# A hand-written instruction order taken two chunks further, across a block border, in a three-layer kernel

## The chip, the cores and the metric

The kernel runs on one core of one Trainium2 chip. Time is device time in microseconds (us) of one execution, the median of several; lower is better.

## The reference

Three layers follow one another over 1,536 tokens of 512 numbers.

```python
# 1: attention, 2 x 8 heads, head size 64: a local window and block maxima as keys
scores_l = scale * np.matmul(q, k.transpose(0, 1, 3, 2))   # kept where |i - j| < 16
scores_s = scale * np.einsum('bhsd,bhnd->bhsn', q, k_sum) + np.log(32)
a = np.exp(scores_all - max);  a = a / (a.sum(-1) + 1e-9)
x = np.matmul(a, v_all)
# 2: dense layer with ELU, 512 -> 2048 -> 512
h = x @ w_in
g = np.where(h > 0.0, h, np.exp(np.minimum(h, 0.0)) - 1.0)
x = g @ w_out
# 3: top-1 of 8 experts, 512 -> 1024 -> 512, weighed by a softmax gate and a sigmoid gate
e_idx = np.argmax(x @ w_gate, axis=1)
out[mask] = gate_w * eom * (np.maximum(x[mask] @ w1[e], 0.0) @ w2[e])
```

## The kernel before, in words

The attention works in 24 units of 64 tokens. A unit is a chain: scores on TensorE (line 330), their maxima on VectorE (340), exp on ScalarE (353), sums, reciprocal (`add_eps` 385, `recip` 391) and norm (401), a turn on TensorE (412), its copy on ScalarE (419), and the product with v on TensorE (449). From the product, which lies in PSUM, ScalarE takes the high part of x (`x_hi`, 455) and VectorE the low part (`x_lo`, 462). From unit 8 on two units go through the chain together.

The dense layer works in four blocks of tokens, 512, 256, 384 and 384 wide, each made of the units that lie in it (8, 4, 6 and 6). Each block goes through 16 chunks of 128 of the 2,048 hidden numbers. A chunk is `mm_h` (line 482: twelve matmuls, high and low parts of x against high and low parts of the weights), `elu` (two passes on ScalarE at 495, two on VectorE at 502 and 508), the split of the result into `gh` (518, ScalarE) and `gl` (524, VectorE), the split of the chunk's output weights (`w_high` 175 on ScalarE, `w_low` 179 on VectorE), and `mm_y` (543), which adds the chunk into one PSUM bank for each 128 tokens: four banks in block 0, two in block 1. TensorE takes `mm_y` two chunks behind `mm_h`. When a block's last `mm_y` is done, `out_y` copies the banks out and stores them. Below, h(j,c) and Y(j,c) are `mm_h` and `mm_y` of block j, chunk c.

During block 0 the weights come in as 64-bit numbers and are put together as fp32: `load_w` (122), `conv_r` (130 and 134, ScalarE), `conv_t` (146, 147 or 149, VectorE), `conv_f` (156, VectorE, for chosen chunks GpSimd), and for w_in `conv_h` (162, ScalarE) and `conv_l` (167, VectorE). The means of v that the units from 12 on need are summed on VectorE (`mean_v1`, 239), go to DRAM and back by DMA, and are put at the top of v by `v_pad` (255). GpSimd has the short copies of k, some norms, and the constants of the routing (`route_consts`, 758 to 793): a load `rc` and some casts, which nobody reads before the first block's tokens are routed.

What sets the order. Until the end of block 0, all engines and the load queue (SP) follow one list, the string `START`, whose tokens are steps: a letter for the step and digits for the unit or chunk. `G` and `H` are `mm_h`, `Y` is `mm_y`, `U` and `V` are the two halves of `elu`, `g` and `f` the split of g, `i` and `j` that of the output weights, `t` the turn, `o` the product, `h` and `l` the parts of x, `F` and `K` sums, `L` a load. Small tables say which engine takes a step: `NE` (norm), `WE` and `KE` (copies of k), `PADA` (units whose `v_pad` is ScalarE's), `CP` (`conv_f` on GpSimd), `EXP` (subtraction of maxima on GpSimd), `RADD` (`add_eps` on GpSimd), `BITS` (w_in chunks converted by a shorter way on ScalarE and a longer one on VectorE). After block 0, TensorE's order is the order of a loop over the steps (`part1`); the table `PAIRS` gives for each pair of units from 12 on the half step at which its chain begins (two half steps a chunk, block 1 has 32 to 63). The other engines then take what a scheduler by priority gives them. The experts at the end are planned apart from that.

Of the kernel before, what the change touches and what calls it, by code (L numbers as in the profile page):

```python
# [13 lines left out]
U32 = mybir.dt.uint32  # L14
# [8 lines left out]
E, F2 = 8, 1024  # L23
# [17 lines left out]
QS = (0, 2, 6, 8)  # L41
C3 = 2
WARM = 56
BITS = (0, 1, 2, 3, 6, 8)
PAIRS = {12: 35, 14: 45, 16: 54, 18: 65, 20: 74, 22: 83}
AT = (2, 6, 8, 8)
LQ = 5
ER = 13
# [33 lines left out]
class Prog:  # L82
# [42 lines left out]
    def conv_r(self, c, part):  # L125
# [13 lines left out]
    def conv_t(self, c, part):  # L139
# [112 lines left out]
    def v_pad(self, u):  # L252
# [363 lines left out]
    def part1(self):  # L616
# [22 lines left out]
        steps = [(j, c) for j in range(NBLK) for c in range(NF)]  # L639
        todo = {}  # L640

        def at(hs, fn, *args):
            todo.setdefault(hs, []).append((fn, args))

        for j in range(2, NBLK):
            for n in range(UNITS[j]):
                u = U0[j] + n
                h0 = PAIRS[u - n % 2]
                if UPB <= u < UPB + self.NKV:
# [27 lines left out]
        h0 = 2 * NF * (NBLK - 1)  # L677
# [39 lines left out]
    def start_up(self):  # L717

        unit = dict(k=self.k_sum, s=self.scores, m=self.maxes, b=self.less_max, e=self.weights, z=self.sums, r=self.recip, R=self.recip2, n=self.norm, t=self.turn_of, c=self.turned,
                    o=self.weighted, h=self.x_hi, l=self.x_lo, p=self.v_pad, x=self.max_k0, w=self.window, a=self.add_eps, M=self.mean_v0, P=self.pad_v0, K=self.red_sum, F=self.mean_v1, Z=self.keep_warm)  # L720
        load = dict(k=self.load_k0, Q=self.load_q0, V=self.load_v0, W=self.load_kw, c=self.load_c, w=self.load_w, q=self.load_q, v=self.load_v, s=self.load_sum, u=self.load_v1)
        part = dict(A=self.conv_r, B=self.conv_t, C=self.conv_f, D=self.conv_h, E=self.conv_l)
        chunk = dict(U=self.elu_act, V=self.elu_dve, Y=self.mm_y, g=self.g_high, f=self.g_low, i=self.w_high, j=self.w_low)
        half = set()
        for u in range(NV):
            self.unit0(u)
        with self.tc.manual_schedule():
            for op in START.split():
# [838 lines left out]
```

## Time and profile before

| | |
|---|---|
| three runs | 526.79, 528.25 and 529.17 us, median 528.25 |
| the profiled execution | 526.98 us, of which 525.2 us are the span of the trace |
| TensorE (PE) busy | 511.6 us, 97% of the span |
| VectorE (DVE) busy | 337.1 us, 64% |
| ScalarE (ACT) busy | 305.1 us, 58% |
| GpSimd (POOL) busy | 54.4 us, 10% |

The shares are means over stages that differ: attention and the start of the dense layer until about 41 us, the rest of block 0 until about 131, block 1 until about 192, then blocks 2 and 3 with the routing, and the experts. They are to be read by stage. A timeline row gives start, duration, engine, line, operation and tiles, and in brackets the engine's idle time before it with what ended it.

### The profile page before, as it was taken

To read this page: it belongs to the slowest core of one execution; us is meant where nothing else is said; L and a number is where in the kernel's file an instruction comes from. 1 tells how busy PE (TensorE), PEld (TensorE's weight loads), DVE (VectorE), ACT (ScalarE), POOL (GpSimd) and SP (SyncE) were. 2 spreads that over 40 slices of the span, in tenths; PEclk is the share of its full clock that TensorE was granted. 3 is DMA by queue.
4 is the path that set the end of the run, shared out by engine and by line. 5 is a ranking of instruction groups with operands and counts; after the bars stand their busy time and mean duration, and the time that the engine had idled before them with its cause. 6 is when DMAs were issued, how large, how long until landed. Compare 5 with 4: busy or idle time off the path is not lost. (4 is left out here: it accounts for less than half of the span.)

```text
span 525.2 us, 9833 instructions
## 1 busy us (share of the span) xinstructions
PE 511.6 (97%) x3325; PEld 409.6 (78%) x3325; DVE 337.1 (64%) x945; ACT 305.1 (58%) x715; POOL 54.4 (10%) x102
## 2 busy tenths in 40 slices
PE   9999999998999999999999999999999999999994
PEld 6486778886888889888898897987888567576883
DVE  5899999997688868676557899668321011535410
ACT  3899998994677658656546547543232223656421
POOL 3530000001000000000000000113411111100001
PEclk9999999999999999999999999999999999999998
DMA  8999334551311212200001025310689898594601
GB/s 293 405 396 331 119 118 140 179 195 50 132 32 52 81 45 78 82 0 16 2 0 62 1 75 192 96 61 1 183 319 302 297 360 317 174 344 149 203 22 43
DMA packets 37131, 78.08 MB, mean 149 GB/s; under 512 B 3951, under 2 KB 9807, under 8 KB 37072
## 3 DMA queue, kind: packets, MB, share of 16 engines
q1 hardware_dynamic: 34752, 70.02, 39.2%
q0 software_dynamic: 2320, 7.34, 4.0%
q8 instruction: 28, 0.46, 0.4%
q14 instruction: 31, 0.25, 0.2%
HBM read 100.37 MB, written 6.55 MB: 204 GB/s over the span
## 5 line engine op out<-in xcount | busy, mean ns | idle before, releaser
L482 PE MATMUL h<-xh,wi 128*128 128x384 f32 (+2 forms) x528 | 142.8, 338 | 2.5 <-DVE elp L508 1.5
L543 PE MATMUL y<-wsp,gh 128*128 128x512 f32 x368 | 117.3, 400 | 0.0
L482 PEld LDWEIGHTS h<-xh,wi 128*128 128x128 f32 x528 | 94.5, 190 | 10.7 <-DVE elp L508 2.4
L482 PE MATMUL h<-xl,wi 128*128 128x384 f32 (+2 forms) x264 | 87.9, 333 | 1.6 <-DVE xl L462 1.6
L543 PEld LDWEIGHTS y<-wsp,gh 128*128 128x128 f32 x368 | 66.8, 190 | 12.3 <-issue 0.5
L543 PE MATMUL y<-wsp,gl 128*128 128x512 f32 x184 | 72.5, 394 | 0.0
L1222 DVE TENSOR_TENSOR holdl<-S,holdh 128x512 fp32r<-128x512 f32 x22 | 15.2, 690 | 72.5 <-ACT holdh L1218 53.7
L1190 PE MATMUL h<-w2s,holdh 128*128 128x512 f32 x176 | 59.8, 400 | 0.0
L1233 PE MATMUL y<-w2s,holdh 128*128 128x512 f32 x176 | 59.0, 398 | 0.0
L482 PEld LDWEIGHTS h<-xl,wi 128*128 128x128 f32 x264 | 50.2, 190 | 5.6 <-DVE xl L462 1.8
L502 DVE SCALAR_TENSOR_TENSOR elt<-ele,elt 128x384 f32<-128x384 f32 (+2 forms) x64 | 35.5, 554 | 24.6 <-ACT ele L495 24.3
L495 ACT ACTIVATE elt<-h 128x384 f32<-128x384 f32 (+2 forms) x64 | 31.2, 487 | 31.1 <-PE h L482 30.5
L175 ACT CAST wsp<-wo 128x512 fp32r<-128x512 f32 x62 | 38.0, 617 | 16.8 <-PE y L543 16.0
L179 DVE TENSOR_TENSOR wsp<-wo,wsp 128x512 fp32r<-128x512 f32 x62 | 42.6, 689 | 6.3 <-ACT wsp L175 6.0
L518 ACT CAST gh<-elp 128x384 fp32r<-128x384 f32 (+2 forms) x62 | 31.5, 508 | 23.5 <-DVE elp L508 12.8
L524 DVE TENSOR_TENSOR gl<-elp,gh 128x384 fp32r<-128x384 f32 (+2 forms) x62 | 34.0, 549 | 12.2 <-ACT gh L518 11.9
L543 PEld LDWEIGHTS y<-wsp,gl 128*128 128x128 f32 x184 | 34.7, 188 | 8.0 <-DVE gl L524 0.3
L353 ACT ACTIVATE e<-e,nb 128x120 f32<-128x120 f32 x88 | 33.6, 385 | 10.8 <-DVE nb L340 10.8
L1233 PEld LDWEIGHTS y<-w2s,holdh 128*128 128x128 f32 x176 | 33.1, 188 | 8.4 <-issue 1.6
L1190 PEld LDWEIGHTS h<-w2s,holdh 128*128 128x128 f32 x176 | 33.1, 188 | 8.2 <-ACT w2s L1258 0.8
L1264 DVE TENSOR_TENSOR w2s<-wo,w2s 128x512 fp32r<-128x512 f32 x48 | 30.8, 687 | 9.3 <-ACT w2s L1258 7.8
L508 DVE SCALAR_TENSOR_TENSOR elp<-elt,h 128x384 f32<-128x384 f32 (+2 forms) x64 | 35.1, 548 | 0.9
(290 smaller groups left out, 819.8 us busy)
## 6 DMA issues: line engine op xcount, KB each, us to landing
wo<-in_w SPq DMA_DIRECT2D x9, 2048.0 KB
wo<-in_w SPq DMA_DIRECT2D x18, 1024.0 KB
ri<-in_w_in SPq DMA_DIRECT2D x16, 512.0 KB
ro<-in_w_out SPq DMA_DIRECT2D x16, 512.0 KB
wo<-in_w SPq DMA_DIRECT2D x32, 256.0 KB
w2p<-in_w SPq DMA_DIRECT2D x32, 256.0 KB
w2q<-in_w SPq DMA_DIRECT2D x24, 256.0 KB
k<-in_kw SPq DMA_DIRECT2D x18, 192.0 KB
```

What stands on the lines that cost most here:

```text
L175: self.nc.scalar.copy(w[:, 0], self.w[c, 1].bitcast(F32))
L179: self.nc.vector.tensor_tensor(w[:, 1], self.w[c, 1].bitcast(F32), w[:, 0].bitcast(F32), op=ALU.subtract)
L353: nc.scalar.activation(e[:, p], e[:, p], AF.Exp, bias=nb[:, p:p + 1], scale=-1.0, accum_out=sm[:, p:p + 1])
L482: nc.tensor.matmul(h, lhsT=w[:, wl, k * 128:k * 128 + 128], rhs=x[:, k, a:b], start=(n == 0), stop=(n == 11))
L495: self.nc.scalar.activation(self.te[j, c][i], self.h[j, c], AF.Exp if i else AF.Tanh, scale=1.0 if i else 0.5)
L502: nc.vector.scalar_tensor_tensor(t, e, 1.0, t, op0=ALU.add, op1=ALU.mult)
L508: nc.vector.scalar_tensor_tensor(p, t, 0.0, h, op0=ALU.min, op1=ALU.max)
L518: self.nc.scalar.copy(gh, p)
L524: self.nc.vector.tensor_tensor(gl, p, gh.bitcast(F32), op=ALU.subtract)
L543: nc.tensor.matmul(self.y[j][t], lhsT=gx[:, sl], rhs=wx, start=(c == 0 and n == 0), stop=(c == NF - 1 and n == len(ops) - 1))
L1190: nc.tensor.matmul(self.h[s, hf], lhsT=x[:, k], rhs=w, start=(n == 0), stop=(n == 11))
L1233: nc.tensor.matmul(self.y2[s], lhsT=g[:, ks], rhs=w, start=(i == 0 and n == 0), stop=(i == 7 and n == 2))
```

## The change

- `START` is written anew, over its whole length. It goes on past block 0: h(1,0) and h(1,1) with their `elu` and splits, Y(0,14), Y(0,15) and the four parts of block 0's `out_y` (`O`) are now tokens of it. Digits are read to base 36, so that `g` and `h` are chunks 0 and 1 of block 1 (`Gg`, `Gh`). The loop begins two steps later (`FIXED = 2`).
- Y(0,13) (`Yd`), which stood ahead of the product of the last units of block 1 (`ob`), now stands behind it, ahead of h(1,0).
- `route_consts` was left to the scheduler; it is now the token `X`, behind the exp of units 10 and 11.
- `PAIRS` moves units 12 to 17 later by four, two and one half steps. Units 16 and 17 then have their product just ahead of Y(1,13), which is followed by h(2,0).
- The tables of engines change. GpSimd takes three norms and two `conv_f` instead of two norms, one `conv_f` and two subtractions of maxima; ScalarE takes two more `v_pad` and, `BITS` being shorter by one, one more pass of `conv_r`.

```diff
-BITS = (0, 1, 2, 3, 6, 8)
-PAIRS = {12: 35, 14: 45, 16: 54, 18: 65, 20: 74, 22: 83}
+BITS = (0, 1, 2, 3, 12)
+PAIRS = {12: 39, 14: 47, 16: 55, 18: 65, 20: 74, 22: 83}
...
-WE = "APPPPA"
-KE = "PVVVVPPP"
+WE = "AAPPPP"
+KE = "VPVPVAPP"
...
-EXP = (3, 4)
-NE = "VVVPVVPV"
-RADD = (0, 2, 3, 4, 6)
-PADA = (3,)
-CP = ((0, 0),)
+EXP = ()
+NE = "PPVVPVVV"
+RADD = (2, 3, 4, 5, 6, 7)
+PADA = (1, 4, 6)
+CP = ((1, 0), (3, 0))
...
+FIXED = 2
...
-        at(2 * NF, self.route_consts)
...
-            for i in range(NF, len(steps)):
+            for hs in range(2 * NF, 2 * NF + 2 * FIXED):
+                run(hs)
+            for i in range(NF + FIXED, len(steps)):
                 run(2 * i)
...
-                n = [int(i, 16) for i in op[2 if k == "L" else 1:]]
+                n = [int(i, 36) for i in op[2 if k == "L" else 1:]]
...
+                elif k == "X":
+                    self.route_consts()
+                elif k == "O":
+                    self.out_y1(0, *n)
...
-                    self.mm_h(0, *n, TB // 2 if n[0] in half else 0)
+                    if n[0] == NF:
+                        self.new_x(2)
+                    self.mm_h(n[0] // NF, n[0] % NF, TB // 2 if n[0] in half else 0)
                 elif k in chunk:
-                    chunk[k](0, *n)
+                    chunk[k](n[0] // NF, n[0] % NF, *n[1:])
```

TensorE where block 0 goes over into block 1, before. `S<-et,v_100` is the product of units 10 and 11 (`ob`), `xh_167` and `xl_168` are the high and low part of x of block 1, `h<-` is h(1,0), `y<-` Y(0,13). A row with xN stands for N instructions in a row.

```order
L543 MATMUL y<-wsp,gh 128x512 x2
L543 MATMUL y<-wsp,gl 128x512
L449 MATMUL S<-et,v_100 64x64 x8
L482 MATMUL h<-xh_167,wi_545 128x256
L482 MATMUL h<-xl_168,wi_545 128x256
L482 MATMUL h<-xh_167,wi_545 128x256 x2
L482 MATMUL h<-xl_168,wi_545 128x256
```

And with the change:

```order
L450 MATMUL S<-et,v_100 64x64 x8
L544 MATMUL y<-wsp,gh 128x512 x2
L544 MATMUL y<-wsp,gl 128x512
...
L483 MATMUL h<-xh_167,wi_397 128x256
L483 MATMUL h<-xl_168,wi_397 128x256
L483 MATMUL h<-xh_167,wi_397 128x256 x2
```

The pair of `y<-` rows stands there four times: all twelve matmuls of Y(0,13) have moved from ahead of the product to between it and the first matmul that reads its result.

VectorE around `x_lo` of units 10 and 11 (`xl_168`) at the same place, before (`wsp<-` is `w_low`, `gl<-` the low part of g, `vs<-` and `ks<-` are sums, `v<-pad` is `v_pad`):

```order
L179 TENSOR_TENSOR wsp<-wo,wsp 128x512 x2
L239 TENSOR_REDUCE vs<-vn_1660 96x16
L179 TENSOR_TENSOR wsp<-wo,wsp 128x512
L524 TENSOR_TENSOR gl<-elp,gh 128x512
L179 TENSOR_TENSOR wsp<-wo,wsp 128x512
L462 TENSOR_TENSOR xl_168<-S,xh_167 128x4x128
L255 TENSOR_SCALAR v_98<-pad 24x512
```

And with the change:

```order
L157 ISA wo<-cv_t,cv_r 128x1024
L525 TENSOR_TENSOR gl<-elp,gh 128x512
L503 SCALAR_TENSOR_TENSOR elt<-ele,elt 128x512
L463 TENSOR_TENSOR xl_168<-S,xh_167 128x4x128
L180 TENSOR_TENSOR wsp<-wo,wsp 128x512
L509 SCALAR_TENSOR_TENSOR elp<-elt,h 128x512
L228 TENSOR_REDUCE ks_97<-kst 128x12
L240 TENSOR_REDUCE vs<-vn_1688 96x16
```

The last `w_low` of block 0, its last `gl`, its last `elp` and the sums, some of which stood ahead of `x_lo`, stand behind it; the last `conv_f`, a `gl` and an `elt` are now directly ahead of it.

GpSimd at the routing constants (`wg`, `r_wg`, `tri`, `val`), before; `rr<-sm` is `add_eps` and `e<-e,rr` a norm, both of units of block 0:

```order
L385 TENSOR_SCALAR rr<-sm 128x4
L771 CAST wg_1743<-rc 128x4x16
L777 CAST tri<-rc 128x128
L783 COPY val<-rc 128x12
L784 COPY val<-rc 128x12
L774 TENSOR_TENSOR r_wg_1745<-rc,wg_1743 128x64
L771 CAST wg_1743<-r_wg_1745 128x4x16
L385 TENSOR_SCALAR rr<-sm 128x4 x2
L774 TENSOR_TENSOR r_wg_1745<-r_wg_1745,wg_1743 128x64
L771 CAST wg_1743<-r_wg_1745 128x4x16
L401 TENSOR_TENSOR e<-e,rr 128x480
```

And with the change:

```order
L157 TENSOR_TENSOR cv_t<-cv_t,cv_r 128x512
L402 TENSOR_TENSOR e<-e,rr 128x480
L386 TENSOR_SCALAR rr<-sm 128x4
L306 COPY k<-ks_96 128x96
L386 TENSOR_SCALAR rr<-sm 128x4
L306 COPY k<-ks_96 128x96
L157 TENSOR_TENSOR cv_t<-cv_t,cv_r 128x512
L306 COPY k<-ks_96 128x96 x2
L779 CAST wg_1391<-rc 128x4x16
L782 TENSOR_TENSOR r_wg_1393<-rc,wg_1391 128x64
```

The casts that stood among block 0's `add_eps` and norms now stand behind all of them. On the load queue `rc` moves in the same way, from 19th to a place behind the weights; the first chunk of w_in moves from the 15th load to the 12th (4.6 MB up to its end instead of 5.5), the second from the 18th to the 19th (7.1 MB instead of 6.6), and chunk 3 from the 22nd to the 29th (10.8 MB instead of 8.4).

## Rows read from the trace of the kernel before

**Rows 1.** Windows by stage: length, then busy us (and instructions) of PE, PEld, DVE, ACT, POOL.

```profile
core 0: us, PE busy (x) PEld busy (x) DVE busy (x) ACT busy (x) POOL busy (x), PEclk, DMA share, GB/s
9.90:41.48 31.58, 29.37 (x396) 19.91 (x395) 28.46 (x118) 27.12 (x84) 13.34 (x30) 1.00 1.04 394
41.48:125.30 83.82, 83.82 (x424) 65.26 (x424) 81.72 (x181) 76.48 (x158) 1.32 (x2) 1.00 0.52 167
125.30:129.24 3.94, 1.45 (x21) 1.12 (x21) 3.50 (x6) 1.50 (x3) 0.00 (x0) 1.00 0.19 56
129.24:132.65 3.41, 3.41 (x15) 3.12 (x14) 1.69 (x5) 0.66 (x2) 0.00 (x0) 0.50 0.03 7
```

**Rows 2.** Waits of PE, 9.5 to 200 us: total, times, longest.

```profile
PE h L482 <- DVE xl L462: 1.6, 1, 1.6
PE T L412 <- POOL e L401: 1.1, 1, 1.1
PE h L482 <- ACT xh L455: 0.9, 1, 0.9
PE h L482 <- DVE elp L508: 0.8, 2, 0.5
```

**Rows 3.** Timeline of PE at the border of blocks 0 and 1.

```profile
125.30 0.69 PE L449 MATMUL S<-et,v 120*64 120x64 f32 x16
...
128.85 0.39 PE L482 MATMUL h<-xl,wi 128*128 128x256 f32 x1 [1.61 <-DVE xl L462]
```

**Rows 4.** Timeline of DVE at the same place.

```profile
125.72 0.68 DVE L239 TENSOR_REDUCE vs<-vn 96x16 f32<-96x512 f32 x1
...
128.12 0.68 DVE L462 TENSOR_TENSOR xl<-S,xh 128x512 fp32r<-128x512 f32 x1
130.92 1.08 DVE L255 TENSOR_SCALAR v<-pad 24x512 f32<-24x512 f32 x3 [2.12 <-DMA pad<-vs]
```

**Rows 5.** Timeline of PE: start of a Y chunk of block 0, and of what follows it.

```profile
118.45 0.61 PE L543 MATMUL y<-wsp,gh 128*128 128x512 f32 x2
...
121.17 0.60 PE L412 MATMUL T<-c,e 128*120 128x128 f32 x4
```

**Rows 6.** Timeline of POOL, 13 to 30 us.

```profile
16.96 0.98 POOL L363 TENSOR_TENSOR e<-e,nb 128x480 f32<-128x480 f32 x1
...
22.34 0.34 POOL L771 CAST wg<-rc 128x64 bf16<-128x64 f32 x1 [3.54 <-DMA rc<-in_rc]
...
25.54 0.98 POOL L401 TENSOR_TENSOR e<-e,rr 128x480 f32<-128x480 f32 x1
26.49 1.28 POOL L156 TENSOR_TENSOR cv_t<-cv_t,cv_r 128x512 int32<-128x512 int32 x1
...
29.05 1.27 POOL L401 TENSOR_TENSOR e<-e,rr 128x480 f32<-128x480 f32 x1 [0.36 <-DVE rr L391]
```

**Rows 7.** Timeline of DVE, 15.5 to 26 us.

```profile
16.80 0.22 DVE L385 TENSOR_SCALAR rr<-sm 128x4 f32<-128x4 f32 x1
...
17.15 0.82 DVE L385 TENSOR_SCALAR rr<-sm 128x4 f32<-128x4 f32 x1
...
19.18 0.43 DVE L146 TENSOR_SCALAR cv_t<-ri 128x512 int32<-128x512 int32 x1 [0.45 <-DMA ri<-in_w_in]
```

**Rows 8.** Timeline of PE: the last scores before h(0,2), and its first matmul.

```profile
40.69 0.26 PE L330 MATMUL T<-k,q 64*64 64x120 f32 x1
41.48 0.47 PE L482 MATMUL h<-xh,wi 128*128 128x512 f32 x1 [0.53 <-DVE elp L508]
```

**Rows 9.** Groups of ACT, 9.9 to 125.3 us: busy us, mean ns.

```profile
L134 ACT ACTIVATE cv_r<-ri 128x512 bf16<-128x512 f32 x10 | 7.8, 783 | 0.0
...
L200 ACT COPY wo<-wo 24x512 f32<-24x512 f32 x1 | 0.6, 614 | 0.0
```

**Rows 10.** Waits of ACT, 40 to 75 us: its only one.

```profile
ACT wsp L175 <- DVE wo L156: 0.3, 1, 0.3
```

**Rows 11.** Timeline of ACT at the border of blocks 1 and 2: `x_hi`.

```profile
189.39 0.59 ACT L429 CAST xh<-S 128x512 fp32r<-128x512 f32 x1
```

**Rows 12.** Timeline of DVE at the same place: `x_lo`.

```profile
190.01 0.69 DVE L462 TENSOR_TENSOR xl<-S,xh 128x512 fp32r<-128x512 f32 x1
```

More of the change, by code (lines that the diff above doesn't have):

```diff
@@ L54 @@
 LG = ((6, 3, 4), (6, 4, 3), (5, 2, 2))
-WE = "APPPPA"
-KE = "PVVVVPPP"
+WE = "AAPPPP"
+KE = "VPVPVAPP"
 EXD = (3, 4)
-EXP = (3, 4)
-NE = "VVVPVVPV"
-RADD = (0, 2, 3, 4, 6)
-PADA = (3,)
-CP = ((0, 0),)
-START = "Lk2 Lk0 w02 Lk3 w43 Lk1 w13 x2 w42 w11 Lc0 x0 x3 w03 w20 w12 w23 w10 w50 x1 w30 w51 w53 LQ0 LQ1 Lc1 LV4 LV1 w01 w00 LW7 w22 k5 k3 w52 k1 k2 s0 s1 w21 k4 m0 s2 w32 s5 m1 m5 k0 w33 LV0 w40 m2 LW6 w41 e0 w31 M7 e1 s3 e5 s4 LV2 Lw00 m4 M2 LV3 LQ2 Lw10 M3 M0 a0 M1 e2 r0 m3 n0 t0 c0 r1 M5 M4 b4 M6 Lwd0 k7 b3 r5 k6 n1 t1 Lw01 a2 Lw30 e4 B00 n5 e3 A00 z4 P r2 c1 A10 s6 s7 z3 n2 a3 t5 p1 p0 p2 o0 c5 Lw50 r3 t2 B10 m6 p3 a4 r4 Lw51 h0 n3 l0 c2 o1 Z2 t3 e6 m7 p4 n4 c3 C00 Lq9 a6 o2 h1 Z8 o3 h2 D0 r6 Lw20 n6 h3 t4 C10 l2 Lwe0 o5 c4 l1 e7 Lw40 l3 E0 p7 t6 h5 Lw11 Lq8 B30 k8 H0 k9 r7 n7 c6 D1 p6 o4 A20 Lwf0 B20 t7 c7 o6 E1 h4 o7 C20 A30 Lw21 l5 l4 h6 h7 l6 Lw60 l7 B01 Lwa0 H1 D2 C30 G0 G1 A01 E2 C01 Lva Lw80 D3 U01 p8 Lv9 U02 E3 V01 V02 A11 B21 A21 B11 Ls00 C11 s8 C21 s9 U11 B51 B40 U12 Lqb i2 V11 A40 m8 A51 Lv8 V12 kb C40 G2 U21 Y0 Lw70 K00 Lqa D4 m9 U22 Lw31 C51 A50 B50 V21 Lwc0 A60 E4 G3 e8 V22 Y1 C50 A31 g2 j2 D5 B60 B31 C60 f2 Lw41 C31 U31 D6 E5 U32 B41 V31 ka Lw61 Ls11 E6 V32 i3 B70 A41 G4 C41 A70 K11 j3 U41 g3 U42 Y2 Lw71 G5 e9 A80 B80 V41 f3 V42 i5 U51 C70 g4 Y3 D7 R8 C80 n9 B61 Ls20 Lw90 D8 E7 E8 U52 Lwb0 V51 n8 G6 t8 A61 V52 Ba0 Aa0 U61 t9 C61 Ls01 i4 Ca0 U62 g5 c8 f4 Da G7 K20 V61 A90 j4 K01 i6 V62 c9 j5 B90 j6 f5 o8 Y4 B71 U71 Lw81 U72 A71 g6 o9 C90 Ea Ab0 V71 f6 Bb0 C71 Cb0 B81 Y5 Ls31 G8 D9 A81 V72 Db h8 E9 g7 U81 C81 Lw91 i7 l8 Eb K31 Y6 j7 Lu0 Ad0 U82 Bd0 f7 i8 B91 G9 V81 Cd0 A91 V82 j8 F0 Lu1 C91 U91 Y7 U92 sa g8 Lu5 V91 Lwa1 Lwb1 Bc0 V92 Ac0 ma F1 Dd f8 Ga F5 sb Y8 g9 Gb Cc0 Ba1 Ls30 ea Ua1 i9 Ua2 mb Va1 Aa1 eb f9 j9 K30 Ed Ra Va2 Ab1 Dc Bb1 Ub1 Ca1 Cb1 Ub2 ga Ec Lwc1 Y9 Ae0 Lu7 ia Lu2 Be0 Vb1 Gc na Vb2 Ce0 Ac1 Uc1 F7 ja Uc2 Ls21 De gb Bc1 Gd fa Cc1 Af0 ib Vc1 Bf0 F2 Vc2 ic Ee K21 Ud1 Lwd1 Ud2 Ad1 Lvb fb Ya jb Ge Lwf1 ta Yb Cf0 Bd1 Df Vd1 Ls10 Cd1 Vd2 jc Ef gc Lwe1 Af1 Bf1 Gf fc Ue1 nb Yc tb ca Ue2 gd id Lu6 Cf1 Ve1 F6 Ve2 if Lu4 K10 jd Lu3 fd Ae1 Uf1 Uf2 oa cb ge F3 Be1 Vf1 Yd Ce1 ie ob Vf2 fe je jf gf ha F4 ff la"
@@ new lines @@
+EXP = ()
[3 more added lines that the diff above has]
+CP = ((1, 0), (3, 0))
+START = "Lk3 x3 w13 Lk0 w03 w30 w53 x0 w50 Lk2 Lk1 w12 w02 w22 LQ0 x2 w00 x1 w20 k4 w01 w11 w52 w23 Lc0 s0 k1 w10 k3 s1 w32 k2 w21 w33 LQ1 Z2 s2 LV4 w42 k0 m0 k5 w51 w40 m1 e0 Lc1 s5 LV1 LV2 w41 e1 m5 Lw00 m2 e5 w43 LW7 LV0 r0 A00 M7 s4 w31 LQ2 s3 M3 m4 LW6 LV3 n0 Lw01 e2 M4 Lw10 r1 M2 B00 m3 t0 c0 b4 b3 n1 M5 a5 k6 a2 r5 C00 M0 r2 Lw90 M1 e3 e4 k7 D0 n5 z3 M6 P t1 c1 n2 p1 z4 s7 a3 Lw20 p0 s6 t5 B10 o0 o1 A10 c5 p4 Lq9 t2 p3 r3 m6 Lw70 a4 r4 h0 h1 C10 n3 m7 c2 e6 n4 B01 p7 p2 Z8 t3 o5 l1 c3 t4 Lq8 a6 e7 Lw50 o2 r6 Lw11 c4 h2 l0 o3 k8 n6 h3 o4 E0 t6 h5 a7 D1 r7 l2 k9 l3 H0 Lw30 h4 c6 n7 A20 p6 t7 Lw60 c7 Lw40 o6 B20 Lw21 o7 E1 C20 s8 B30 s9 Lw51 Lqa Lwa0 A30 h6 h7 D2 l5 l4 l6 l7 A01 G0 C30 D3 U01 E2 Lw80 B11 U02 C01 E3 Ls00 Lwf0 H1 V01 G1 V02 A11 A21 B21 U11 U12 G2 C11 K00 B50 C21 Lw41 A40 Y0 A50 V11 B40 V12 U21 C40 Lqb D4 Lv9 i2 U22 C50 m9 ka e9 m8 G3 A51 V21 E4 e8 V22 A41 Y1 U31 B41 B51 j2 C41 g2 D5 Lw31 Lv8 C51 Lw61 f2 G4 B31 E5 Y2 A31 U32 C31 V31 V32 i3 A60 B60 g3 j3 C60 f3 U41 G5 D6 U42 B61 E6 Lwb0 Lw91 V41 R8 V42 Y3 B70 A61 A70 n8 Lwc0 U51 C70 U52 g4 Lva Ls20 G6 n9 i5 V51 t9 K20 V52 D7 E7 A90 t8 C61 B80 i4 j4 G7 f4 A80 c8 Y4 C80 j5 B90 U61 D8 p8 C90 Lw71 U62 g5 V61 D9 Ls01 f5 o8 V62 E8 Ab0 Lwd0 kb Lwe0 Bb0 K01 c9 Cb0 U71 Y5 i6 Aa0 G8 U72 Ba0 Lw81 j6 g6 Ca0 V71 f6 E9 A71 B71 o9 Db V72 h8 U81 Eb C71 Y6 B81 g7 U82 Bd0 l8 V81 i7 A81 G9 f7 j7 Lvb Da Y7 Ea C81 Lwa1 Ad0 A91 Cd0 V82 Ac0 Bc0 i8 g8 B91 sb Cc0 U91 j8 C91 f8 U92 V91 i9 Aa1 sa Ls21 Ga V92 Dc Ua1 Dd g9 mb ma Lwb1 Ed Ec Y8 Ua2 j9 f9 K21 Va1 Va2 ea X eb Ra Gb Lwd1 Ab1 Y9 Lwe1 Ba1 Gc Ub1 Ca1 Ub2 Bb1 nb ga Vb1 ia Vb2 na Ae0 Be0 ja Uc1 Uc2 Cb1 ta Ce0 ca fa Bf0 Vc1 Af0 Cf0 De ib Gd Ya Ad1 gb Vc2 Lu5 Ee gc Bd1 Ls11 Cd1 Ge fb Df Ud1 F5 Lwc1 jb Be1 tb Ae1 Ef cb Lwf1 K11 Ud2 Ce1 Bc1 Vd1 Vd2 Yb oa Ac1 Lu3 Cc1 Ue1 Gf fc gd ic id jc Lu0 Bf1 Yc Ue2 fd Af1 Ve1 Ve2 Lu4 F3 jd Lu6 Uf1 Uf2 ge F4 ob ha Cf1 fe Yd Vf1 la ie Gg Lu7 if je Ls10 Vf2 Ls31 ih K10 F6 Ye F0 Ug1 ig gf Lu1 jf ff Ls30 Ug2 Vg1 Vg2 gg F1 Yf Gh K31 jh O0 fg Lu2 jg O1 F7 K30 O2 O3 F2 Uh1 Uh2 Vh1 Vh2"
@@ L698, in part1 @@
         with self.tc.manual_schedule(engines={mybir.EngineType.PE}):
-            for i in range(NF, len(steps)):
+            for hs in range(2 * NF, 2 * NF + 2 * FIXED):
+                run(hs)
+            for i in range(NF + FIXED, len(steps)):
                 run(2 * i)
                 j, c = steps[i]
-                if c == 0 and 1 <= j < NBLK - 1:
+                if c == 0 and 2 <= j < NBLK - 1:
                     self.new_x(j + 1)
@@ L705, in part1 @@
                 self.split_w(j, c)
-                if i > NF:
+                if i >= NF + FIXED:
                     self.split_g(*steps[i - 1])
```

## The prediction

> **What bounds the kernel now.** I read the stages first: windows cut at the borders of the blocks. In block 0, from 41.48 to 125.30 us, TensorE is busy for all of its 83.82 us, VectorE for 81.72 and ScalarE for 76.48 [rows 1]. So TensorE sets the time, the other two follow with little to spare, and work taken off them pays only where TensorE waits for them. Where it waits is the second view, its list of waits: from the start of the attention to the end of block 1 there are four kinds that matter, together 4.4 us [rows 2]. Two of them, 0.9 us for `x_hi` and 1.6 us for `x_lo`, fall in one place, the border between block 0 and block 1. The third view is that place on two engines: the product of units 10 and 11 is the last thing before h(1,0) [rows 3], ScalarE and VectorE still have to take x from it, and on VectorE four other operations that were started or ready run from 125.72 to 128.12 us ahead of `x_lo` [rows 4]. After the border comes a stretch of 3.41 us in which TensorE is busy without a gap but its granted clock is 0.50, the 1.2 GHz level, behind 3.94 us in which it had been busy for only 1.45 [rows 1]. The two waits are thus paid for once more.
>
> **The change, part by part.** The sum is made against the profiled execution, 526.98 us; the median of the three runs, 528.25, is 1.27 above it.
>
> *The border, -4.2 us.* It costs 0.9 + 1.6 = 2.5 us of waits [rows 2] and half of 3.41 us at half the clock, 1.7 us [rows 1]. With the change the twelve matmuls of Y(0,13) stand between the product and h(1,0). Such a chunk takes 121.17 - 118.45 = 2.72 us [rows 5]. What has to fit under it: `x_hi` and `x_lo`, which took 0.59 + 0.69 us at the next border [rows 11, 12], so 1.3 us if both engines are free. ScalarE has nothing between that could not run earlier. VectorE has the last `conv_f`, a `gl` and an `elt` directly ahead of `x_lo`, 0.68 us each by the row of its neighbours [rows 4]. If none of the three has begun when the product ends, `x_lo` ends 4 x 0.68 = 2.7 us after it, just as h(1,0) wants it; all three can run earlier, since their inputs come from chunk 15's h, which ends a whole Y chunk and a product ahead (2.72 + 0.69 us). I take no wait left. The other bound: two more operations of VectorE's late, 1.4 us, and a clock that falls as it does now, 1.7 us; that leaves -4.2 + 3.1 = -1.1 us. TensorE's matmuls are the same in number, so nothing is added there. Block 0's copies of y (`O`) bring no wait as I see it: h(1,1) and h(1,2) lie between Y(0,15) and Y(1,0), which needs the banks, twelve matmuls of 256 columns each, so half of 2.72 us each, against copies that I put at 0.6 us like the one in [rows 9].
>
> *The start, -1.0 us.* Three edits meet ahead of h(0,2). The constants' casts run on GpSimd from 22.34 us, after it stood 3.54 us for their load [rows 6], and the norm behind them ends so late that TensorE waits 1.1 us for it [rows 2]; with the casts moved to mid-block, where GpSimd has 1.32 us of work in 83.82 [rows 1], this wait goes. At the end of the stage h(0,2) begins at 41.48 us, though the last scores began at 40.69: it waits for `elp` of chunk 0 [rows 8]. A gain counts only as far as it reaches that point, since from there TensorE has no gap. Best case: the 1.1 us and the 0.7 us of that hole (41.48 less 40.69 and some 0.1 to the next issue), -1.8 us. Against it, ScalarE and VectorE are busy 27.12 and 28.46 of the 31.58 us [rows 1], and ScalarE gets work: two `v_pad` at 0.61 and one pass of `conv_r` at 0.78 [rows 9], 2.0 us in all of START, of which I put half in this stage. The worst: that 1.0 us lands in full on h(0,2), +1.0. I take -1.0, nearer to the best end, because the wait of 1.1 us is gone for certain and the loads of the first weights come earlier, as told below. Later in block 0 VectorE must keep up with a TensorE that is 1 us ahead: it has 2.1 us free there [rows 1], and `w_low`, `gl` and `elp` of the last chunk go behind `x_lo`, 2 us less ahead of the border.
>
> On GpSimd, three norms at 0.98 and 1.27 and two `conv_f` at 1.28 come for two norms, one `conv_f` and two subtractions at 0.98 [rows 6]: 5.9 us instead of 5.5. A `tensor_scalar` of VectorE's took 0.82 us beside GpSimd's subtraction, the same shape 0.22 us shortly before [rows 6, 7]. The Trainium skill ("SBUF — State Buffer", "Who interferes with whom") says that such pairs lock each other out for a whole instruction, which agrees with 0.82 against 0.22; by it, VectorE would lose some 0.4 us more than now ahead of h(0,2), an estimate, and the forecast would be 523.6. I leave that out of the sum, because the start's price has wider bounds.
>
> *Block 1, +0.2 us.* Units 12 to 17 begin later. At the border to block 2 only Y(1,13) now covers `x_hi` and `x_lo`: two tiles, half of 2.72 = 1.36 us [rows 5], against 189.39 to 190.70, 1.31 us [rows 11, 12]. Without delay it fits; I put 0.2 for a small one. Bounds: 0, and 0.7 for one operation of VectorE's in between [rows 12]. From block 2 on every engine's order is unchanged: nothing.
>
> Sum: -4.2 - 1.0 + 0.2 = -5.0 us, 522.0 for a profiled execution; as a median 528.25 - 5.0 = **523.2 us**. The bounds of start and block 1 give 522.2 (-4.2 - 1.8) to 525.7 (-4.2 + 1.0 + 0.7).
>
> **The rivals.**
>
> *ScalarE becomes the bound in block 0.* From 40 to 75 us it waits for 0.3 us in all [rows 10], so work that is moved into that stretch delays `gh` and `xh` at once. For it: the 2.0 us of new work. Against it: over the block it is busy 76.48 of 83.82 us, and VectorE's part is done earlier. If the 2.0 us show up on TensorE and the start gives nothing, -4.2 + 2.0 + 0.2 = -2.0: 526.2 us.
>
> *The border's wait is replaced.* `v_pad` waited 2.12 us for a DMA at the border [rows 4], and only `x_lo` stood ahead. It stands among block 1's first steps now; VectorE does what it is told in order, so a late sum or DMA holds up `gl` of the next chunks. Or `x_lo` itself is late, as bounded above. Either costs 1.4 us and the clock's 1.7: -1.1 - 1.0 + 0.2 = -1.9: 526.3 us. For it: VectorE is the fuller engine. Against it: sums and loads are put further ahead of their reader.
>
> *The loads set the start: slower.* From 9.9 to 41.48 us the DMA moves 394 GB/s with its engines full [rows 1], so a load lands when the bytes ahead of it are through. VectorE met its first weights with a wait of 0.45 us at 19.18 [rows 7]. With the change chunk 0 has 0.9 MB less ahead, 2.3 us; but its conversions stand in the orders of ScalarE and VectorE at a place that I estimate at 15.4 to 15.9 us, adding up today's durations of what stands ahead, so they wait 1 us, or up to 3.3 if the weights land no earlier than now. Chunk 1 comes 0.5 MB later (1.3 us), chunk 3 by 2.4 MB (6 us), and both conversions are asked for earlier than now, for which I allow up to 1.5 and 2.0 us. Both engines stand at the same loads, so if none of this is idle time that they had anyway, 6.8 us reach h(0,2). Then -4.2 + 6.8 + 0.2 = +2.8: 531.0 us. It decides from 4.0 us together on. Against it: the two engines have 3 to 4.5 us of idle time in the stage, and the list has loads spread out otherwise.
>
> That the change does not do what it says is no case of its own: the orders of TensorE and GpSimd show both moves.
>
> **How the numbers follow.** The forecast, within its own range of 522.2 to 525.7, gets 0.70: its largest term is read off rows and its cover is twice what it hides. ScalarE as the bound 0.13, a replaced wait 0.11, the loads 0.06. A measurement of this kernel tells about 0.5%, 2.6 us, from no change. The forecast gives faster, 0.70; ScalarE and the replaced wait gain 2 us, which is the same, 0.24; the loads slower, 0.06. The range goes from 521.4, 0.8 below the best sum since runs differ by 1 us to either side, to 526.8, which takes in both rivals at 526; it leaves out the loads and the tails.
>
> **What would show it.** Right, if h(1,0) follows Y(0,13) with no wait for `xh` or `xl` and no window near there has the clock at 0.50; if the turn at 26 us waits for no norm; if h(0,2) begins at 39.7 to 40.8 us; and if TensorE's time from there to h(1,1) is some 4 us shorter. Waits of TensorE for `gh` or `xh` between 45 and 75 us would speak for ScalarE, waits for `xl`, `gl` or a low clock in the first 10 us of block 1 for the replaced wait, waits of both engines at lines 130 and 146 before 35 us with h(0,2) after 41.5 for the loads. The forecast is wrong if block 0's own time from h(0,2) on grows by over a microsecond.

## The result and the profile after

The changed kernel is slower. Ten runs of each gave a median of 529.94 us against 526.68 before; the ratio is 1.0058, with a 95% interval of 1.0039 to 1.0077, so 3.1 us (2 to 4) lost where 5 were forecast as a gain. The profiled execution of the changed kernel has a span of 528.9 us against 525.2.

TensorE's waits from the start of the attention to the end of block 1, in the changed kernel (total, times, longest; lines from 76 to about 660 are numbered one higher than before):

```profile
PE S L331 <- issue: 3.1, 2, 1.7
PE h L483 <- DVE elp L509: 2.8, 3, 1.3
PE y L331 <- DMA wo<-in_q: 0.9, 1, 0.9
PE T L413 <- ACT et L420: 0.8, 1, 0.8
PE y L605 <- DVE mc L595: 0.6, 1, 0.6
...
PE h L483 <- DVE xl L463: 0.4, 1, 0.4
```

Against [rows 2], the waits for the norm (1.1 us), for `xh` (0.9) and for `xl` at the border (1.6) are gone; the 0.4 us for `xl` are of the first block. In their place there are two waits of the scores, 3.1 us, which name no releaser, and three for `elp`, of 0.43 us in block 0 and of 1.33 and 1.06 in block 1. The windows by stage, cut at h(0,2), at the end of the product of units 10 and 11, at the end of h(1,0), at h(1,1) and at h(2,0), and one stretch in the experts (columns as in [rows 1]):

```profile
9.90:41.76 31.86, 29.29 (x395) 19.83 (x395) 27.05 (x116) 27.43 (x85) 12.35 (x27) 1.00 0.99 359
41.76:124.42 82.66, 82.16 (x430) 63.31 (x429) 76.67 (x169) 75.82 (x155) 3.36 (x12) 1.00 0.51 169
124.42:128.70 4.28, 4.28 (x28) 3.79 (x25) 3.01 (x5) 2.15 (x4) 0.00 (x0) 1.00 0.64 184
128.70:134.17 5.47, 5.47 (x26) 4.49 (x25) 5.38 (x11) 3.70 (x8) 0.00 (x0) 1.00 0.24 73
134.17:194.85 60.68, 54.60 (x546) 48.59 (x544) 49.24 (x165) 40.42 (x128) 2.89 (x8) 1.00 0.23 72
353.00:356.00 3.00, 3.00 (x11) 2.09 (x10) 1.38 (x10) 0.38 (x2) 0.00 (x0) 0.50 0.00 1
```

The border is as forecast: TensorE busy without a gap, the clock at 1.00. Its idle time now lies in block 1, 60.68 - 54.60 = 6.1 us between h(1,1) and h(2,0): 3.1 us in the two waits of the scores, 2.4 in two for `elp`, and 0.6 for `mc`, an operand of the routing. Four landmarks on TensorE, the start of a first matmul each, say how much each stage cost; the work between them is the same in the four kernels but for the order (the last two are experiments, below):

| kernel | h(0,2) | h(1,0) | h(2,0) | last matmul | h(1,0) to h(2,0) |
|---|---|---|---|---|---|
| before | 41.48 | 126.86 | 192.20 | 518.14 | 65.34 |
| changed | 41.76 | 127.27 | 194.85 | 521.83 | 67.58 |
| border and constants only | 40.33 | 124.57 | 186.56 | 513.82 | 61.99 |
| changed, loads mended | 40.08 | 126.08 | 193.50 | 519.26 | 67.42 |

Before, block 1 took 65.34 us with the border's wait for `xl` and the stretch at half the clock in it, 1.6 + 1.7 us; without them it would have been 62.0, which the third kernel has. The changed kernel needs 67.58 without either. So block 1 lost 5.6 us of its own. The start gave nothing (0.3 us later at h(0,2)). After h(2,0) the change has 1.0 us more. There TensorE has a stretch at half the clock, from 352.8 to 356.1 us, which the profiled execution of before does not have; the one of the fastest kernel below has such a stretch too (from 344.1 to 347.5 us; it takes 327.26 us behind h(2,0)), so it isn't the change's.

The border in detail, on TensorE and VectorE:

```profile
123.80 0.69 PE L450 MATMUL S<-et,v 120*64 120x64 f32 x16
...
127.27 0.28 PE L483 MATMUL h<-xh,wi 128*128 128x256 f32 x1
```

```profile
123.74 0.68 DVE L157 CUSTOM_DVE_ANT_0 wo<-cv_t,cv_r 128x1024 uint16<-128x1024 uint16 x1
124.34 0.69 DVE L525 TENSOR_TENSOR gl<-elp,gh 128x512 fp32r<-128x512 f32 x1
124.95 0.68 DVE L503 SCALAR_TENSOR_TENSOR elt<-ele,elt 128x512 f32<-128x512 f32 x1
125.55 0.68 DVE L463 TENSOR_TENSOR xl<-S,xh 128x512 fp32r<-128x512 f32 x1
```

`x_lo` is done by 126.2 us, a microsecond before h(1,0) wants it; `conv_f`, `gl` and `elt` stand ahead of it as the order said.

What was not foreseen is this place in block 1, on TensorE, ScalarE and VectorE:

```profile
158.29 1.15 PE L450 MATMUL S<-et,v 120*64 120x64 f32 x32
...
161.09 0.28 PE L331 MATMUL S<-k,q 64*64 64x120 f32 x1 [1.65 <-issue]
```

```profile
159.68 0.59 ACT L430 CAST xh<-S 128x512 fp32r<-128x512 f32 x1
```

```profile
160.30 0.69 DVE L463 TENSOR_TENSOR xl<-S,xh 128x512 fp32r<-128x512 f32 x1
```

The product of units 12 and 13 is written into the PSUM bank `S`. The scores of units 14 and 15 are the next thing on TensorE, and want the same bank: the pool `psa` has one buffer for each name. They start at 161.09 us, 0.1 us after `x_lo` has taken the product out (160.30 + 0.69). The same happens with the next pair, whose product starts at 176.34 us:

```profile
178.95 0.28 PE L331 MATMUL S<-k,q 64*64 64x120 f32 x1 [1.46 <-issue]
```

A product comes eight half steps after its pair's begin (`AT`), and the new `PAIRS` are 39, 47, 55: eight apart, so that each product falls into the half step in which the next pair's scores are issued. Before they were 35, 45, 54.

### The profile page after: what moved, and what is told of

It is laid out like the page before. It is cut to its first block, busy times and chain, and to the rows that moved or that the text cites. A ratio compares the mean times of both kernels' runs of the same rounds, so it can differ in the third digit from the quotient of the medians.

```text
span 528.9 us, 9829 instructions
## 1 busy us (share of the span) xinstructions
PE 510.4 (97%) x3325; PEld 409.1 (77%) x3325; DVE 336.3 (64%) x940; ACT 306.8 (58%) x719; POOL 54.8 (10%) x103
## 5 line engine op out<-in xcount | busy, mean ns | idle before, releaser
L1198 PE MATMUL h<-w2s,holdh 128*128 128x512 f32 x176 | 61.1, 408 | 0.0
```

What stands on the lines that cost most here:

```text
L1198: nc.tensor.matmul(self.h[s, hf], lhsT=x[:, k], rhs=w, start=(n == 0), stop=(n == 11))
```

## The experiments

Each kernel had 6 to 12 executions. Before was run beside them, and a ratio is against those runs (medians 528.25 us for 1 to 4, 527.72 for 5 to 8, 527.75 for 9 to 11).

**1. The changed kernel with the old PAIRS.**

```diff
-PAIRS = {12: 39, 14: 47, 16: 55, 18: 65, 20: 74, 22: 83}
+PAIRS = {12: 35, 14: 45, 16: 54, 18: 65, 20: 74, 22: 83}
```

> The changed kernel with the old PAIRS (35, 45, 54) and all else of the change. Theory A: in the changed kernel the product of units 12 and 13 stands in the same half step as the scores of units 14 and 15 (47), and that of 14 and 15 with the scores of 16 and 17 (55); both want the one PSUM bank S, so the scores wait for x_hi and x_lo, 1.65 and 1.46 us. With the old numbers these two waits go: 3.3 us less than the changed kernel, about 526.6 us. Theory B: block 1's loss of 6 us comes from the end of START (copies of y and sums ahead of elu of h(1,1), h(1,3) waits 1.3 us): no more than 1 us less, about 529.

535.07 us, ratio 1.0130 (1.0106 to 1.0154): slower than the change, against both theories. The two waits of the scores behind a product are gone, but others came. TensorE's list has

```profile
PE h L483 <- DVE elp L509: 5.0, 3, 4.2
PE S L331 <- POOL k L306: 2.4, 1, 2.4
```

and VectorE shows why `elp` is late:

```profile
142.59 1.08 DVE L256 TENSOR_SCALAR v<-pad 24x512 f32<-24x512 f32 x3 [2.05 <-DMA pad<-vs]
```

The new START has the last sums (`K`, `F`) behind the border. The copies of k for units 12 and 13 and the DMA that carries the means of v are late by that, and VectorE stands before `v_pad` with the maxima and `elp` behind it. So the move of `PAIRS` belongs to the new START: its late sums ask for late pairs, and late pairs, with block 2's border fixed, are eight apart.

**2. Before, with the new PAIRS alone** (the reverse of that edit, in the kernel before).

> The kernel before with the new PAIRS (39, 47, 55) alone. Theory A: two new waits of the scores, without a releaser that the profile names, 3.3 us in all: about 530 us against 526.7. Theory B: within 1 us of before.

532.16 us, ratio 1.0075 (1.0050 to 1.0100), 3.9 us slower: theory A. The two waits are 1.46 us each, so 1 us of the price lies elsewhere: the profiled execution also has a wait of 0.9 us for the weights of a late chunk of block 0.

It shows one more thing. The border is the old one here, with both of its waits, and TensorE's clock stays at 1.00 behind them, where before went to 0.50:

```profile
128.59 0.39 PE L482 MATMUL h<-xh,wi 128*128 128x256 f32 x1 [0.87 <-ACT xh L455]
130.53 0.39 PE L482 MATMUL h<-xl,wi 128*128 128x256 f32 x1 [1.55 <-DVE xl L462]
```

```profile
131.00:135.00 4.00, 4.00 (x25) 3.51 (x24) 1.84 (x5) 0.94 (x3) 0.00 (x0) 1.00 0.02 6
```

So the stretch at half the clock follows these waits in one execution and not in another.

**3. Before, with the border alone turned round.**

```diff
-nb Yc tb ca
+nb tb Yc ca
...
-oa cb ge F3 Be1 Vf1 Yd Ce1 ie ob Vf2 fe je jf gf ha F4 ff la
+cb oa ob ge ha F3 Be1 Vf1 Yd Ce1 ie Vf2 la fe je jf gf F4 ff
```

> The kernel before with only the border of blocks 0 and 1 turned round: product of units 10 and 11 ahead of Y(0,13), x_hi and x_lo moved forward accordingly, all else as it was. If the border is worth what its two waits and the stretch at half the clock show: 3.3 to 4.2 us less than before, 522.5 to 523.4, and no window at 0.50 clock near 130 us. If the gain is swallowed in block 1 by ScalarE and VectorE being late: 526 to 527.

524.62 us, ratio 0.9921 (0.9896 to 0.9946): 3.6 us by the medians, 4.2 by the ratio. The border's price came out, and VectorE had the time for it with all its sums where they were.

**4. The changed kernel with Y(0,13) back ahead of the product.**

```diff
-ge F4 ob ha Cf1 fe Yd Vf1 la ie Gg
+ge F4 Yd ob ha Cf1 fe Vf1 la ie Gg
```

> The changed kernel with Y(0,13) put back ahead of the product (x_lo behind elt as in the change). The border theory: x_hi and x_lo uncovered, 1.3 to 2 us of waits and a stretch at half the clock, 1.7 us: 533 us or so against 529.9. If the cover was no part of the change's effect: 530.

531.34 us, ratio 1.0060 (1.0039 to 1.0081), where the changed kernel had 1.0058: no difference that can be told. The 533 us of the border theory were not reached, and the trace says by what. On TensorE:

```profile
127.75 0.38 PE L483 MATMUL h<-xh,wi 128*128 128x256 f32 x1 [0.69 <-ACT xh L456]
128.47 0.39 PE L483 MATMUL h<-xl,wi 128*128 128x256 f32 x1 [0.34 <-DVE xl L463]
```

Without the cover the waits are 1.0 us, not 2.5, since nothing stands ahead of `x_lo` any more (VectorE is idle for 2.24 us before it), and no stretch at half the clock follows: windows from 126.8 to 137 us have it at 1.00, which by number 2 may be chance. Most of the border's waits, 1.5 of 2.5 us, came from the four operations ahead of `x_lo` [rows 4], and less from TensorE's order.

**5. Before, with pairs eight apart but not late.**

```diff
-PAIRS = {12: 35, 14: 45, 16: 54, 18: 65, 20: 74, 22: 83}
+PAIRS = {12: 37, 14: 45, 16: 53, 18: 65, 20: 74, 22: 83}
```

> The kernel before with PAIRS 37, 45, 53 alone: pairs eight half steps apart as in the change, but the last one a half step earlier than before, not later. Theory A (the bank S: product and next scores in one half step): two waits of the scores of 1.4 to 1.7 us each, 3 to 4 us slower than before. Theory C (what costs is that the chain of units 12 to 17 is late): no slower than before, within 1 us.

531.91 us, ratio 1.0081 (1.0054 to 1.0108). Theory A: the last pair is earlier than before, so its lateness is no part of it; the first is two half steps later than before, which this run leaves open. TensorE's list:

```profile
PE S L330 <- issue: 3.3, 2, 1.8
PE h L482 <- DVE xl L462: 1.8, 1, 1.8
```

**6. The changed kernel with pairs nine apart** (`PAIRS` 37, 46, 55).

> The changed kernel with PAIRS 37, 46, 55: the product of a pair and the scores of the next are one half step apart, with a Y chunk of 1.4 us between. Theory A: both waits of the scores, 1.65 and 1.46 us, all but go; v_pad stands two half steps earlier and may wait for its DMA for 1 us or so: about 527 us against 529.9. Theory C: the last pair is as late as in the change, so 530.

528.88 us, ratio 1.0029 (1.0006 to 1.0052), so about 1.5 us of the change's loss is mended, half of what was expected. No wait of the scores for the bank is left, but others came; the one for a copy of k is the earlier pairs meeting the late sums, and what brought on the other two kinds was not taken apart:

```profile
PE h L483 <- DVE elp L509: 2.6, 4, 0.8
PE y L605 <- DVE mc L595: 1.5, 2, 1.1
...
PE S L331 <- POOL k L306: 0.8, 1, 0.8
```

**7. Before, with the routing constants alone moved** to `X` behind `eb`, as in the change.

> The kernel before with the routing constants alone moved to mid-block. If the norm behind the casts is what bounds the start: the wait of 1.1 us goes and h(0,2) begins up to 1 us earlier, 0.5 to 1.1 us less than before. If VectorE bounds h(0,2) anyway: the wait goes and h(0,2) begins where it did, within 0.3 us of before.

525.55 us, ratio 0.9956 (0.9936 to 0.9977), 2.2 us less than before, more than either expectation. The profiled execution shows half of that: h(0,2) begins at 40.43 us instead of 41.48, behind the same wait for `elp`:

```profile
40.43 0.47 PE L482 MATMUL h<-xh,wi 128*128 128x512 f32 x1 [0.52 <-DVE elp L508]
```

The hole there is no limit of its own: the whole chain in front of it moved up by the microsecond that the norm had cost.

**8. Before, with border and constants** (3 and 7 together).

> The kernel before with the border turned round as in the third run and the routing constants moved: the two parts of the change that take waits away, without the parts that move loads, sums and pairs. The third run's 3.6 us less, and 0 to 1.1 us more from the constants: 3.6 to 4.7 us less than before.

521.66 us, ratio 0.9882 (0.9854 to 0.9910), 6.1 us less than before and the best kernel of this study. That is more than the 3.6 to 4.7 expected, since the constants alone gave more; the two add up. TensorE's list for the same 190 us is short:

```profile
PE h L482 <- DVE elp L508: 0.8, 2, 0.5
PE y L330 <- DMA wo<-in_q: 0.3, 1, 0.3
PE T L412 <- ACT et L419: 0.2, 1, 0.2
```

**9. That kernel with START taken on into block 1**, in the manner of the change but with the sums, tables and `PAIRS` of before: behind `ff` follows

```
Gg Ye Ug1 ig Ug2 Vg1 jg Vg2 gg Yf Gh fg O0 ih O1 Uh1 O2 Uh2 jh O3 Vh1 Vh2
```

> The kernel of the run with border and constants, with the first two chunks of block 1, the last two Y of block 0 and its copies of y taken into START as in the change, the old tables and PAIRS and the sums left where they were. If a fixed order past the border is itself a cost (h(1,3) waiting for elp of h(1,1) for 1.3 us as in the changed kernel): 1 to 3 us slower than the run with border and constants, so 2.5 to 5 us less than before. If the cost in the change was that sums, their loads and v_pad were put behind that tail: as fast as that run within 0.7 us, about 6 us less than before.

525.50 us, ratio 0.9967 (0.9943 to 0.9990): 3.8 us slower than number 8, a little more than the 1 to 3 expected. So the tail as it is written is a cost without the late sums too. On the landmarks 2.9 us of it lie in block 1 (64.84 us from h(1,0) to h(2,0) against 61.99). There it has a wait that number 8 doesn't have:

```profile
143.84 0.39 PE L483 MATMUL h<-xh,wi 128*128 128x256 f32 x1 [1.78 <-DVE elp L509]
```

This is h(1,4), which waits for the `elp` of h(1,2). On ScalarE the exps of units 12 and 13 stand ahead of what that `elp` needs, and on VectorE their two norms and two more operations come before it:

```profile
136.90 0.42 ACT L354 ACTIVATE e<-e,nb 128x120 f32<-128x120 f32 x1
...
140.22 0.39 ACT L496 ACTIVATE elt<-h 128x256 f32<-128x256 f32 x1
```

In the changed kernel it is another chunk, h(1,3), on TensorE and, with what VectorE does between the `elp` of h(1,0) and that of h(1,1), there:

```profile
140.36 0.39 PE L483 MATMUL h<-xh,wi 128*128 128x256 f32 x1 [1.33 <-DVE elp L509]
```

```profile
135.59 0.68 DVE L556 TENSOR_SCALAR m<-y 128x512 f32<-128x512 f32 x1
136.19 0.68 DVE L240 TENSOR_REDUCE vs<-vn 96x16 f32<-96x512 f32 x1
136.79 0.54 DVE L228 TENSOR_REDUCE ks<-kst 128x12 f32<-128x384 f32 x1
...
139.90 0.41 DVE L509 SCALAR_TENSOR_TENSOR elp<-elt,h 128x256 f32<-128x256 f32 x1
```

The bank of h(1,1) is free when this `elp` is done, and h(1,3) wants it. The exps that h(1,1) needs from ScalarE were done at 136.5 us; a copy of y, the late sums and splits of output weights stood ahead.

The tail also changes TensorE's own order, which the list of the edits did not say: Y(0,14) and Y(0,15) now both stand ahead of h(1,1), where the loop takes h(1,1) between them. Before, h(1,1) and then Y(0,15):

```profile
134.56 0.28 PE L482 MATMUL h<-xh,wi 128*128 128x256 f32 x1
...
137.06 0.73 PE L543 MATMUL y<-wsp,gh 128*128 128x512 f32 x2
...
143.09 0.37 PE L482 MATMUL h<-xh,wi 128*128 128x256 f32 x1
```

Changed, the end of Y(0,15) and then h(1,1):

```profile
133.94 0.39 PE L544 MATMUL y<-wsp,gl 128*128 128x512 f32 x1
134.17 0.28 PE L483 MATMUL h<-xh,wi 128*128 128x256 f32 x1
```

From the start of h(1,1) to that of h(1,3) before had 143.09 - 134.56 = 8.5 us, in which the `elp` of h(1,1) had to be done; the changed kernel, without its wait, has 140.36 - 1.33 - 134.17 = 4.9 us. Number 9 has this order too. How much of the tail's price comes from it, and how much from the fixed order on the other engines, no run here separates.

**10. The changed kernel with the start's loads mended**: the first chunk's conversions one unit later, and the loads of chunks 3 and 9 exchanged.

```diff
-r0 A00 M7 s4 w31 LQ2 s3 M3 m4 LW6 LV3 n0 Lw01 e2 M4
+r0 M7 s4 w31 LQ2 s3 M3 m4 LW6 LV3 n0 Lw01 e2 A00 M4
...
-B00 m3
+m3 B00
...
-Lw90
+Lw30
```

> The changed kernel with the first chunk's two conversions (A00, B00) moved behind the next unit's exp and maxima and the load of chunk 3 exchanged with that of chunk 9. If the waits for the loads (1.63 and 0.52 us on ScalarE, 1.36 and 0.80 on VectorE) took away the start's gain: those waits mostly go and h(0,2) begins at 40.4 to 40.8 us instead of 41.8, 1 to 1.4 us less than the changed kernel, 528.5 or so. If the new tables of engines cost it: h(0,2) stays within 0.4 us of 41.5.

h(0,2) begins at 40.08 us instead of 41.76, so the loads were what had eaten the start's gain. In the changed kernel ScalarE and VectorE both stand at the first weights:

```profile
17.76 0.79 ACT L131 ACTIVATE cv_r<-ri 128x512 uint16<-128x512 uint32 x1 [1.63 <-DMA ri<-in_w_in]
```

```profile
17.76 0.43 DVE L147 TENSOR_SCALAR cv_t<-ri 128x512 int32<-128x512 int32 x1 [1.36 <-DMA ri<-in_w_in]
```

and with the mend only this is left of VectorE's waits for them:

```profile
DVE cv_t L147 <- DMA ri<-in_w_in: 0.4, 1, 0.4
```

The time hardly follows: 529.88 us, ratio 1.0047 (1.0026 to 1.0068), whose interval holds the change's own 1.0058. By the landmarks 0.5 us of the 1.7 are lost again by h(1,0) and the rest holds to the end; runs of this kernel spread over 4.7 us, and the profiled one is the shortest of them. It also has no stretch at half the clock in the experts.

**11. Both mends together** (10, with `PAIRS` 37, 46, 55).

> The changed kernel with both mends, loads as in the run before this one and PAIRS 37, 46, 55. If they add up: 1.5 for the pairs and 1 to 1.4 for the loads, 527 us or so, as fast as before and still 5 us slower than the run with border and constants, because sums and v_pad stay late.

528.05 us, ratio 1.0013 (0.9992 to 1.0034): as fast as before, a microsecond short of the sum, and 6.4 us slower than number 8.

## Why the prediction was wrong

*The step that failed* is "Block 1, +0.2 us". It looked at the one place where the border to block 2 lost its cover, which did fit, and not at what else the new numbers put into one half step. Measured on its own the move of `PAIRS` costs 3.9 us (2), and pairs eight apart with an earlier last one 4.2 (5); both bring back the waits for the bank, 2.9 and 3.3 us, and that is its mechanism. In the changed kernel block 1 lost 5.6 us in place of 0.2: 3.1 us of waits for the bank, the rest for `elp` and `mc`. TensorE's order had shown it, had I gone through block 1 as through the border: a product directly followed by scores. It had shown h(1,1) behind Y(0,15) too, and the term has no price for that (9). And the bounds, 0 and 0.7 us, were made for one reason alone, so they were no bounds.

*The border, -4.2.* Its size came out where it stands alone: 3.6 us by medians, 4.2 by the ratio, with an interval from 2.9 to 5.5 (3). It was wrong in part on the cause: I gave it to TensorE's twelve matmuls; with VectorE's queue shortened, the cover is worth a microsecond of waits (4). And the 1.7 us for the clock were taken as a price that the waits always bring. Of the four profiled executions with the old border, before and number 7 have the stretch at 0.50 behind it, with waits of 2.5 and 2.1 us there; numbers 2 and 5 don't, with 2.4 and 2.7. So that term is a price of some executions. On the mean it seems to have been won: the mean granted clock of before's 69 executions has a median of 0.994, that of the changed kernel's ten 0.998; stretches at other places count in these means too.

*The start, -1.0.* Two effects of opposite sign. The constants alone were worth more than put down: -2.2 us by the medians, at least 1.2 by the interval, and 1.1 by the landmarks, at h(0,2) (7). The loads took it back: +1.4 us at h(0,2) against number 8, shown by 10. That is the rival of the loads, in its place and with its rows, at a fifth of its price of 6.8 us: the first weights landed at 17.7 us, where 19.18 - 2.3 = 16.9 was reckoned from the bytes, and they were waited for by 1.4 to 1.6 us.

*ScalarE as the bound* did not come: in block 0's window it is busy 75.82 of 82.66 us. Block 0 from h(0,2) to h(1,0) takes 85.51 us against 84.24 in number 8; that 1.3 us was not tracked down beyond a wait of 0.4 for `elp` there.

*The replaced wait* happened, though not at `x_lo`, but two chunks on, as the 1.33 us for `elp` at h(1,3). The tail, its order on TensorE included, and the late sums stand ahead of it (9), in shares that no run separates. The cause of the second wait for `elp` in block 1, 1.06 us, stays open.

The slower side was put at 0.06, all on the loads. Most of it came by a mechanism that stood in no case. On the landmarks the changed kernel is behind number 8, which has the two gains and nothing else, by 1.4 us at the start, 1.3 in block 0 and 5.6 in block 1, and 0.3 ahead of it after h(2,0): 8.0 us, where the medians lie 8.3 apart. Against before the same landmarks give 0.3 + 0.1 + 2.2 + 1.0 = 3.7 us for the profiled executions, against 3.1 measured; of these the last 1.0, with the stretch at half the clock in the experts, is chance.

## What to carry to other kernels

When steps move to other slots, list for every slot what else is issued there, and look at which buffers they share: a product and the next scores in one bank cost 3 to 4 us here, though each was in a good place by itself. Take such a change apart before it is judged as a whole: two of its parts were worth 6 us together, and the rest took 9 back. A longer list that is written by hand fixes the order on all engines, also where the loop had a better one: the tail alone cost 3.8 us in number 9, with h(1,1) moved behind Y(0,15) and the other engines' order fixed, in shares that are open.

## What the runs showed of the hardware

The waits for the shared PSUM bank stand in the profile with no releaser ("issue"), 1.65 us long, while TensorE did nothing; the true one is found by the row that ends just before, `x_lo` at 160.99 us against 161.09.

The granted clock does not fall at the same places in every execution. It went to 0.50 behind the border of before, 2.5 us of waits in 3.94 us [rows 1], stayed at 1.00 behind 2.4 us of the same waits in number 2, and stayed there behind the 1.0 us of waits in number 4. In the experts of the changed kernel's profiled execution it went to 0.50 from 352.8 to 356.1 us, with TensorE busy throughout. What the engine did before it fell is this row, 24 narrow matmuls of 16 columns each:

```profile
349.42 2.82 PE L611 MATMUL y<-rc,mt 128*128 128x16 f32 x24
```

Every kernel here has that row, of the same length. In five of the 13 profiled executions (changed, 1, 2, 8 and 9) the clock falls to 0.50 some 3 us after its start, for about as long as in [rows 1]; in the other eight it stays at 1.00 there. What decides between them is open. So one profiled execution can have such a stretch, or lack it, whatever the change did, and a difference of a microsecond or two between two profiles has to be looked at for it first.
